# One x tile turned by the crossbar instead of TensorE, a gate vector read as rows, a later weight load, and another engine at the last wait

## The chip, the core and the metric

The kernel runs on one core of a Trainium2 chip. The core has five engines, each with an instruction list of its own that it works off in order: TensorE (PE, with PEld for its weight loads), VectorE (DVE), ScalarE (ACT), GpSimd (POOL) and SyncE (SP), which only issues transfers. Transfers run on 16 DMA engines that all queues share; SyncE's are q1 in the profile, ScalarE's q10, GpSimd's q0. Engines wait for each other through semaphores. The metric is the device time of one execution in microseconds; smaller is better. The time before is 260.21 us, the median of three runs (259.76 to 260.26).

## The reference

Two blocks read the same `x` (2048 tokens of 640 features, bfloat16), and a gate per token mixes their results:

```python
x = A_x
g = _sigmoid((x * gate_w).sum(-1, keepdims=True))
a = _A_ref(x, A_wqkv, A_wo)                     # linear attention, 32 heads of 20
b = _B_ref(x, B_w1, B_w2, B_w3, B_w4)           # mixer with shifted columns, then an MLP of 1728
return g * a + (1 - g) * b

# A: q, k, v = x @ wqkv;  phi(t) = where(t > 0, t + 1, exp(t)) + 1e-6
#    kv = phi(k)^T v, z = sum phi(k), o = phi(q) kv / (phi(q) z + 1e-6), a = o @ wo
# B: h = gelu(layernorm(x) @ w1); four column groups of h are shifted by 1 or 2 tokens; x1 = x + h_shifted @ w2
#    b = x1 + gelu(layernorm(x1) @ w3) @ w4
```

## The kernel before, in words

The tokens are cut into 16 tiles of 128 (`t`), and four chunks of 512 (`c`); the 640 features into five pieces of 128 (`k`). Everything stays in SBUF. `_Sched` records every operation with what it reads and writes, works out the semaphore waits, and emits one instruction list per engine. The order of the work is set by `_Items.run`, a planner with a cost model: it keeps streams of items (name, duration, dependencies with lags) and always takes the item that could start first on TensorE by its model. An item's function emits its instructions, its transfers too, at that place of the engines' lists.

The stages, in order of time:
- Loads and warm-up. Before the planner starts, the transfers of the beginning are written out by hand: ScalarE's queue loads the first piece of wq; SyncE's loads x tiles 0 to 2, wq's second piece, x tile 3, the other wq pieces, the five pieces of `wkg`, the gate vector, then the x chunks of tiles 4 to 15. TensorE multiplies constants meanwhile.
- Queries and keys of block A. Products need x with features on partitions, `xT`. Tiles 0 to 3 are turned by TensorE (`t_x`: five transposes into PSUM, line 617, and a VectorE copy, line 671), tiles 4 to 15 by the crossbar: a transposing transfer from SyncE's queue (line 703). `q_four` does the queries of tiles 0 to 3 as one stream, whose order of steps is a list written by hand: `(t, k)` is the product of tile t with piece k of wq (lines 893 and 894), `(t, None)` turns tile t. Then `k_first` (line 914) and `k_tile` do the keys; `wkg` has 642 columns read there: the keys' 640, one of ones and one with the gate vector, so that a row sum and the gate's product come with the keys. ScalarE takes exponentials, VectorE finishes phi.
- Block A's small matrices (`gt_step`, line 812, `kvt_group`, `lt_evac`, `m_quads`), and layer norm 1: GpSimd normalizes a tile, SyncE turns it by the crossbar into `xnT`.
- Products with w1 and w2 (`w1_group`, `w2_tile`), layer norm 2 in the same way (`n2`, `t2`: item `("t2", u)` is the transposing transfer of tile u), products with w3 (`w3_group`, `w3_half`, line 1120) and w4 (`w4_enter`, lines 1208 and 1213, `w4_tile`, line 1233), with block A's output products (`a_tile`) in between. Weight loads w3 and w4 are items of the planner on SyncE's queue (`w3_load`, `w4_load`).
- Outputs: transfers to HBM from SyncE's queue and, for a part of the last tile, ScalarE's.

At the end `emit` appends the waits for the outputs' landings to SyncE's list, and a barrier of all engines closes the program. The function `stream` has a case `(None, None)`, which the order of `q_four` does not use before; it held a short warm-up.

Of the kernel before, what the change touches and what calls it, by code (L numbers as in the profile page):

```python
# [5 lines left out]
BF16 = mybir.dt.bfloat16  # L6
F32 = mybir.dt.float32
ACTF = mybir.ActivationFunctionType
# [3 lines left out]
D = 640  # L12
# [3 lines left out]
NT = S // 128  # L16
NCH = S // 512
KD = D // 128
# [33 lines left out]
class _Sched:  # L52
# [247 lines left out]
    def emit(self):  # L300
        nc = self.nc
        with ExitStack() as es:
            sems = {}
            for e in ("pe", "act", "dve", "pool"):
                sems["c:" + e] = es.enter_context(nc.semaphore("cnt_" + e))
            for k in self.dma_cnt:
                sems["d:" + k] = es.enter_context(nc.semaphore("dma_" + k))
            seen = {w for p in self.prog.values() for (waits, _fn, _sem) in p for w in waits}
            last = {k: i for i, k in enumerate(self.out_order)}
            left = [k for k in self.dma_cnt if k not in last and ("d:" + k, 16 * self.dma_cnt[k]) not in seen]  # L310
            for k in sorted(last, key=last.get, reverse=True) + left:
                self.prog["sp"].append(([("d:" + k, 16 * self.dma_cnt[k])], None, None))
            engs = {"pe": nc.tensor, "act": nc.scalar, "dve": nc.vector, "pool": nc.gpsimd, "sp": nc.sync}

            for name, e in engs.items():
                for (waits, fn, sem) in self.prog[name]:
                    for (sk, val) in waits:
                        e.wait_ge(sems[sk], val)
                    if fn is not None:
                        fn(e).then_inc(sems[sem], 16 if sem.startswith("d:") else 1)  # L320
            nc.all_engine_barrier()
# [95 lines left out]
def _build(nc, A_x, A_wqkv, A_wo, B_w1, B_w2, B_w3, B_w4, gate_w, out, dbg=None, stop=None):  # L417
    sch = _Sched(nc)
# [37 lines left out]
    pa = Arena(SB_LO, SB_HI - SHARED)  # L456
# [3 lines left out]
    ps = nc.alloc_psum_tensor("ps", [128, 8, 512], F32)  # L460
# [6 lines left out]
    ident = pa.alloc("ident", [128, 128], BF16)  # L467
# [11 lines left out]
    x_tok = pa.alloc("x_tok", [128, NT, D], BF16)  # L479
# [10 lines left out]
    junk = pa.alloc("junk", [128, 1, D], BF16)  # L490
    qprod = pa.alloc("qprod", [128, D], F32)
    zacc = qprod
    zsum = pa.alloc("zsum", [128, D], BF16)
    zT = ones_c[:, :].rearrange("p (k f) -> p k f", f=128)
    zf = pa.alloc("zf", [128, KD], BF16)
    xT = ra.alloc("xT", [128, KD, S], BF16)
    GT = ra.alias("GT", [128, KD, D], BF16, ra.last_addr, KD * S * 2)
    wkg = ra.alloc("wkg", [128, KD, NK], BF16)
# [21 lines left out]
    def bank():  # L520
        best = None
        for k_ in range(nbanks[0]):
            b = (bank_rr[0] + k_) % nbanks[0]
            if b in bank_pend or b in bank_hold:
                continue
            lk = sch.locks.get(b)
            tfree = 0.0 if lk is None else sch.ev_time.get((lk[1].sem, lk[1].val), 1e18)
            if best is None or tfree < best[0]:
                best = (tfree, b)
        bank_rr[0] = best[1] + 1  # L530
        bank_pend.add(best[1])
        return best[1]
# [67 lines left out]
    def mm_group(out_ap, pairs, reads_extra=()):  # L600
        n = len(pairs)

        def fn(e, out_ap=out_ap, pairs=pairs, n=n):
            ins = None
            for i, (l, r) in enumerate(pairs):
                ins = e.matmul(out_ap, l, r, start=(i == 0), stop=(i == n - 1))  # L606
            return ins
        reads = [a for p in pairs for a in p] + list(reads_extra)
        return pe(fn, reads, [out_ap], cost=n * (max(nfree(pairs[0][1]), 24) * 0.4167 + 2.5))
# [39 lines left out]
    def activation(out_ap, in_ap, func, scale=1.0, bias=0.0, accum=None):  # L649
        rd = [in_ap] + [a for a in (scale, bias) if not isinstance(a, (int, float))]  # L650
        wr = [out_ap] + ([accum] if accum is not None else [])
        n = nfree(out_ap)
        cost = max(150.0, 100.0 + 0.833 * n + (70.0 if in_psum(in_ap) else 0.0)) + 45.0 * (len(rd) - 1)
        if accum is not None:
            cost += 91.0
        st_ = ACT_SET.get(func)
        if st_ is not None and st_ != sch.act_func:
            cost += 1290.0
            sch.act_func = st_
        if accum is not None:  # L660
            return act(lambda e: e.activation(out_ap, in_ap, func, bias=bias, scale=scale, accum_out=accum), rd, wr, cost=cost)  # L661
        return act(lambda e: e.activation(out_ap, in_ap, func, bias=bias, scale=scale), rd, wr, cost=cost)  # L662
# [4 lines left out]
    def copy(engf, out_ap, in_ap):  # L667
        cost = None
        if engf is dve and in_ap.dtype == BF16 and out_ap.dtype == BF16:
            cost = 65.0 + nfree(out_ap) / 1.92  # L670
        return engf(lambda e: e.tensor_copy(out_ap, in_ap), [in_ap], [out_ap], cost=cost)  # L671
# [7 lines left out]
    def dma_in(out_ap, in_ap, key, **kw):  # L679
        return sch.dma("sp", out_ap, in_ap, key, **kw)  # L680
# [4 lines left out]
    def load_wq(k, queue="sp"):  # L685
        sch.dma(queue, wq[:, k, :], A_wqkv[128 * k:128 * (k + 1), 0:D], "wq%d" % k)

    memset(pool, wkg[:, :, D:D + 2], 1.0)
    load_wq(0, "act")
    for t in range(3):  # L690
        load_x(t)
    load_wq(1)
    load_x(3)
    for k in range(2, KD):
        load_wq(k)
    for k in range(KD):
        dma_in(wkg[:, k, 0:D], A_wqkv[128 * k:128 * (k + 1), D:2 * D], "wk%d" % k)
    dma_in(wkg[:, :, D + 1:D + 2], gate_w.rearrange("(k p o) -> p k o", p=128, o=1), "gw", noncontig=True)
    for c in range(1, NCH):
        for u in {1: (1,), 2: (2, 3)}.get(c, ()):  # L700
            dma_in(x_tok[:, 4 * u:4 * u + 4, :], x2[512 * u:512 * (u + 1), :].rearrange("(n p) d -> p n d", p=128), "xc%d" % u)
        for t in range(4 * c, 4 * c + 4):
            sch.dma("sp", xT[:, :, 128 * t:128 * (t + 1)], x_tok[:, t, :], "trx%d" % (t % 4), transpose=True)

    k_done = {}

# [47 lines left out]
    IT = _Items()  # L754
    WARM = 3072
    WARM2 = 128
# [97 lines left out]
    def warmup(cols, cyc):  # L854
        b = bank()
        steps = [512] * (cols // 512) + [128] * (cols % 512 // 128)

        def fn(e):
            ins = None
            for n in steps:  # L860
                ins = e.matmul(ps[:, b, 0:n], one(128), one(n), start=True, stop=True)
            return ins
        pe(fn, [], [ps[:, b, :]], cost=cols * cyc)
# [13 lines left out]
    def stream(order, w, n2, done):  # L877
        bs = {}
        for t, k in order:
            if k is None:  # L880
                if t is None:
                    warmup(WARM2, 0.42)
                else:
                    t_x(t)
                continue
            if k == 0:
                bs[t] = pair()
                bank_hold.update((bs[t], bs[t] + 1))
            b = bs[t]
            l = xT[:, k, 128 * t:128 * (t + 1)]  # L890

            def fn(e, l=l, b=b, k=k):
                e.matmul(ps[:, b, 0:512], l, w[:, k, 0:512], start=(k == 0), stop=(k == KD - 1))  # L893
                return e.matmul(ps[:, b + 1, 0:n2], l, w[:, k, 512:512 + n2], start=(k == 0), stop=(k == KD - 1))  # L894
            pe(fn, [w[:, k, 0:512 + n2], l], [ps[:, b, 0:512], ps[:, b + 1, 0:n2]], cost=272.0)
            if k == KD - 1:
                bank_hold.difference_update((b, b + 1))
                done(t, b)

    def q_four():  # L900
        order = [(0, 0), (1, None), (2, None), (1, 0), (0, 1), (1, 1), (2, 0), (2, 1), (3, None), (0, 2), (1, 2), (0, 3), (0, 4), (1, 3),
                 (1, 4), (2, 2), (2, 3), (2, 4), (3, 0), (3, 1), (3, 2), (3, 3), (3, 4)]
        stream(order, wq, 128, lambda t, b: phi(b, pq_tok[:, t + 1, :]))

    def k_out(t, b):
# [370 lines left out]
    for c in range(NCH):  # L1276
        for j in range(KD):
            deps = [(("t1", u), 0.9) for u in range(4 * c, 4 * c + 4)] if j == 0 else []
# [6 lines left out]
    for t in range(NT):  # L1285
        c = t // 4
        deps = [(("w1", c, KD - 1), GEL)]
# [8 lines left out]
    for u in range(NT):  # L1296
        deps = [(("s2", u // 4), 3.2 + 0.9 * (u % 4))]
# [4 lines left out]
        IT.add("N2", ("n2", u), 0.0, lambda u=u: normalize(2, u, st2), deps)  # L1302
        IT.add("T2", ("t2", u), 0.0, lambda u=u: t_xn(2, u), deps=[(("n2", u), 1.1)])
    IT.add("MISC", ("w3load",), 0.0, w3_load, deps=[(("k", NT - 1), 0.0), (("t1", NT - 1), 0.0)])
    IT.add("MISC", ("w4load",), 0.0, w4_load, deps=[(("kvt",), 0.0), (("t1", NT - 1), 0.0), (("z", NT - 1), 1.5)])
    for c in range(NCH):
        for j in range(KFF):
            deps = []
# [4 lines left out]
            if j == 0:  # L1313
                deps = deps0 + [(("t2", u), 0.9) for u in range(4 * c, 4 * c + 4)]
# [11 lines left out]
    for t in range(NT):  # L1326
        deps = [(("zb",), 1.0), (("qr", max(t // 4, 1)), 2.0)]
# [48 lines left out]
    order = IT.run(sch, hook)  # L1376
# [42 lines left out]
```

## Time and profile before

| What | Value |
|---|---|
| Median of three runs | 260.21 us (259.76 to 260.26) |
| Profiled execution | 260.06 us |
| Span of its trace, first to last instruction | 258.3 us |
| Busy: TensorE, VectorE, ScalarE, GpSimd | 254.8, 158.2, 110.9, 96.8 us |
| Granted TensorE clock | 1.000 |
| Moved by DMA | 26.78 MB |

The span is what the views of the trace divide; the 1.8 us around it are start and end of the program outside its instructions. A timeline row has the start in us, the duration, engine, line, operation, what is written and read, how many instructions are merged, and in brackets the idle time before and who ended it. A DMA row has the median time from issue to landing at its end. A row of the chain is a piece of the path that ended last. A row of a window has, behind the stretch, each engine's busy time and number of instructions, and then the granted clock, the share of the DMA engines' time and GB/s.

### The profile page before, as it was taken

The numbers are of one execution on the slowest core, as the hardware profiler recorded it, in microseconds if no ns is written. First come the engines' busy times: TensorE is split into PE (matmuls) and PEld (weight loads), VectorE is DVE, ScalarE is ACT, GpSimd is POOL, SyncE is SP. The second block draws the span as 40 slices with busy tenths as digits, with TensorE's granted clock in tenths as the row PEclk, the third lists the DMA queues.
The fourth block names the chain that finished last, engine by engine and source line by source line (L and its number), as shares of the span: only waits on it lengthen the run. The fifth ranks groups of instructions, "written<-read, shape, count | busy, mean of one in ns | idle before, by whom it ended". The sixth has DMA issues, their size and how long they took to land.

```text
span 258.3 us, 3824 instructions
## 1 busy us (share of the span) xinstructions
PE 254.8 (99%) x1427; PEld 122.7 (47%) x1427; DVE 158.2 (61%) x293; ACT 110.9 (43%) x229; POOL 96.8 (37%) x154
## 2 busy tenths in 40 slices
PE   7999999999999999999999999999999999999996
PEld 3555555544444554554444444444444444444443
DVE  2597877899954699989995302999022530134076
ACT  1496777751355857684874240005500045200100
POOL 8014996869934119659681210111020120021000
DMA  6857997826527699483668512114200140000224
GB/s 194 263 101 235 139 141 193 231 55 119 102 49 105 124 392 305 82 101 65 127 124 117 102 20 23 25 25 130 42 3 0 20 124 0 0 0 1 43 84 139
DMA packets 58644, 26.78 MB, mean 104 GB/s; under 512 B 49966, under 2 KB 57215, under 8 KB 58626
## 3 DMA queue, kind: packets, MB, share of 16 engines
q1 hardware_dynamic: 57122, 22.92, 42.5%
q0 software_dynamic: 1168, 3.28, 5.4%
q10 hardware_dynamic: 336, 0.35, 0.4%
q8 instruction: 11, 0.18, 0.3%
q14 instruction: 7, 0.06, 0.1%
HBM read 12.09 MB, written 2.67 MB: 57 GB/s over the span
## 4 chain that ended last, share of the span: by engine, by line
PE 97%; DMA 1%; DVE 0%; issue 0%
PE ps L606 61%; PE ps L1233 22%; PE ps L812 7%; PE ps L893 2%; PE ps L792 1%; DMA x_tok<-in_A_x_dram 1%; PE ps L1120 1%; PE ps L1208 1%; PE ps L617 1%; PE ps L914 1%; PE ps L894 0%; PE ps L984 0%; PE ps L793 0%; PE ps L1213 0%; PE ps L1017 0%; DVE xT L671 0%
## 5 line engine op out<-in xcount | busy, mean ns | idle before, releaser
L606 PE MATMUL ps<-xnT,w 128*128 128x512 bf16 x360 | 81.3, 379 | 0.0
L606 PEld LDWEIGHTS ps<-xnT,w 128*128 128x128 bf16 x360 | 34.6, 98 | 39.3
L645 DVE SCALAR_TENSOR_TENSOR x_tok<-ps,stg,abx 128x512 bf16<-128x512 f32 (+2 forms) x17 | 12.2, 718 | 58.5 <-PE ps L1233 58.4
L1233 PE MATMUL ps<-w,h2T 128*128 128x512 bf16 (+2 forms) x221 | 47.2, 366 | 0.0
L628 POOL TENSOR_SCALAR abx<-x_tok,stg 128x512 f32<-128x512 bf16 x16 | 12.0, 753 | 88.2 <-DVE x_tok L645 70.1
L628 POOL TENSOR_SCALAR xn<-x_tok,st 128x640 bf16<-128x640 bf16 x32 | 38.6, 1215 | 8.6 <-DMA xnT<-xn 8.2
L662 ACT ACTIVATE h2T<-ps 128x512 bf16<-128x512 f32 x52 | 29.9, 599 | 22.7 <-PE ps L606 22.6
L1233 PEld LDWEIGHTS ps<-w,h2T 128*128 128x128 bf16 x221 | 21.2, 98 | 24.1
L662 ACT ACTIVATE tlT<-ps 128x512 bf16<-128x512 f32 x8 | 4.8, 597 | 64.1 <-PE ps L606 41.9
L662 ACT ACTIVATE Er<-ps 128x640 bf16<-128x640 f32 (+1 forms) x35 | 22.9, 658 | 17.8 <-PE ps L606 9.7
L661 ACT ACTIVATE junk<-x_tok 128x640 bf16<-128x640 bf16 x32 | 23.6, 737 | 4.7 <-DVE x_tok L643 4.2
L662 ACT ACTIVATE hsT<-ps 128x512 bf16<-128x512 f32 (+1 forms) x32 | 18.9, 593 | 14.2 <-PE ps L606 13.8
L606 PE MATMUL ps<-w,hsT 128*128 128x512 bf16 (+1 forms) x160 | 24.0, 299 | 0.0
L606 PE MATMUL ps<-wkg,xT 128*128 128x512 bf16 (+1 forms) x150 | 22.6, 299 | 0.0
L606 PE MATMUL ps<-M_sb,pqnT 128*128 128x512 bf16 x80 | 19.7, 379 | 0.0
L606 PEld LDWEIGHTS ps<-w,hsT 128*128 128x128 bf16 x160 | 13.4, 98 | 12.5
L645 DVE SCALAR_TENSOR_TENSOR abx<-ps,stg,abx 128x512 f32<-128x512 f32 x16 | 12.0, 750 | 10.7 <-PE ps L606 7.2
L606 PEld LDWEIGHTS ps<-wkg,xT 128*128 128x128 bf16 x150 | 12.6, 97 | 11.7
L643 DVE SCALAR_TENSOR_TENSOR x_tok<-ps,x_tok 128x640 bf16<-128x640 f32 x16 | 13.1, 821 | 7.6 <-PE ps L606 6.9
L812 PE MATMUL ps<-pk_tok,x_tok 128*128 128x512 bf16 x80 | 17.8, 379 | 0.0
L636 DVE TENSOR_TENSOR qprod<-qprod,pk_tok 128x640 f32<-128x640 f32 x13 | 16.3, 1252 | 0.5
L628 DVE TENSOR_SCALAR Er<-Er 128x640 bf16<-128x640 bf16 (+1 forms) x35 | 11.6, 332 | 7.6 <-ACT Er L662 6.8
(85 smaller groups left out, 282.9 us busy)
## 6 DMA issues: line engine op xcount, KB each, us to landing
w<-in_B_w_dram SPq DMA_DIRECT2D x1, 2160.0 KB, 9.5
w<-in_B_w_dram SPq DMA_DIRECT2D x1, 2080.0 KB, 15.0
x_tok<-in_A_x_dram SPq DMA_DIRECT2D x3, 640.0 KB, 5.6
out_dram<-x_tok SPq DMA_DIRECT2D x3, 640.0 KB, 3.5
w<-in_B_w_dram POOLq DMA_DIRECT2D x8, 160.0 KB, 6.2
wkg<-in_A_wqkv_dram SPq DMA_DIRECT2D x5, 160.0 KB, 3.9
wv<-in_A_wqkv_dram POOLq DMA_DIRECT2D x1, 800.0 KB, 5.6
x_tok<-in_A_x_dram SPq DMA_DIRECT2D x4, 160.0 KB, 3.2
```

Source lines behind the costliest of these rows:

```text
L606: ins = e.matmul(out_ap, l, r, start=(i == 0), stop=(i == n - 1))
L617: ins = e.transpose(o, s_, ident[:])
L628: return engf(lambda e: e.tensor_scalar(out_ap, in_ap, s1, s2, op0, op1), rd, [out_ap], cost=cost)
L636: return engf(lambda e: e.tensor_tensor(out_ap, a, b_, op), [a, b_], [out_ap], cost=cost)
L643: return dve(lambda e: e.scalar_tensor_tensor(out_ap, in0, scalar, in1, op0, op1, accum_out=accum), rd, [out_ap, accum], cost=cost + 70.0)
L645: return dve(lambda e: e.scalar_tensor_tensor(out_ap, in0, scalar, in1, op0, op1), rd, [out_ap], cost=cost)
L661: return act(lambda e: e.activation(out_ap, in_ap, func, bias=bias, scale=scale, accum_out=accum), rd, wr, cost=cost)
L662: return act(lambda e: e.activation(out_ap, in_ap, func, bias=bias, scale=scale), rd, wr, cost=cost)
L792: e.matmul(ps[:, b, :], l, x_tok[:, t, 0:512], start=(t == 0), stop=(t == NT - 1))
L812: ins = e.matmul(ps[:, b, :], l, r, start=(t0 + q_ == 0), stop=(t0 + q_ == NT - 1))
L893: e.matmul(ps[:, b, 0:512], l, w[:, k, 0:512], start=(k == 0), stop=(k == KD - 1))
L1233: ins = e.matmul(o, l, r, start=False, stop=(i == KFF - 1), skip_group_check=shared)
```

## The change

There are four parts.
- x tile 3 is turned by a transposing transfer from ScalarE's queue instead of TensorE and VectorE. A one-column exponential ahead of it makes ScalarE load its table first. SyncE's transposes of tiles 4 to 15 wait for it (`deps=[turned3]`). The hand-written order of `q_four` loses `(3, None)`, and `(2, 2)` moves ahead.
- The gate vector is read from ScalarE's queue as five contiguous rows of 128 into a new tile `gw5`, instead of element by element into column 641 of `wkg`. A new step `gate_turn`, fourth in `q_four`'s order, turns it with one TensorE product against the identity, and VectorE copies the result into that column.
- The item that loads w4 waits for other items, `("ms",)` (the M rows sent to HBM) and `("t2", 7)`, instead of `("t1", 15)` and `("z", 15)`, so that it comes later in SyncE's queue.
- The waits for the outputs' landings are appended to GpSimd's list instead of SyncE's.

```diff
             for k in sorted(last, key=last.get, reverse=True) + left:
-                self.prog["sp"].append(([("d:" + k, 16 * self.dma_cnt[k])], None, None))
+                self.prog["pool"].append(([("d:" + k, 16 * self.dma_cnt[k])], None, None))
...
+    gw5 = pa.alloc("gw5", [KD, 128], BF16)
...
     load_wq(0, "act")
+    sch.dma("act", gw5[:, :], gate_w.rearrange("(k p) -> k p", p=128), "gw")
     for t in range(3):
         load_x(t)
...
+    activation(junk[:, 0, 0:1], nc.const_aps.tensor(1.0, [128, 1], BF16), ACTF.Exp)
+    turned3 = sch.dma("act", xT[:, :, 384:512], x_tok[:, 3, :], "tr3", transpose=True)
     for k in range(KD):
         dma_in(wkg[:, k, 0:D], A_wqkv[128 * k:128 * (k + 1), D:2 * D], "wk%d" % k)
-    dma_in(wkg[:, :, D + 1:D + 2], gate_w.rearrange("(k p o) -> p k o", p=128, o=1), "gw", noncontig=True)
...
-            sch.dma("sp", xT[:, :, 128 * t:128 * (t + 1)], x_tok[:, t, :], "trx%d" % (t % 4), transpose=True)
+            sch.dma("sp", xT[:, :, 128 * t:128 * (t + 1)], x_tok[:, t, :], "trx%d" % (t % 4), transpose=True, deps=[turned3])
...
                 if t is None:
-                    warmup(WARM2, 0.42)
+                    gate_turn()
...
+    def gate_turn():
+        b = bank()
+        mm_group(ps[:, b, 0:KD], [(gw5[:, :], ident[0:KD, 0:KD])])
+        copy(dve, wkg[:, :, D + 1:D + 2], ps[:, b, 0:KD].unsqueeze(2))
+
     def q_four():
-        order = [(0, 0), (1, None), (2, None), (1, 0), (0, 1), (1, 1), (2, 0), (2, 1), (3, None), (0, 2), (1, 2), (0, 3), (0, 4), (1, 3),
-                 (1, 4), (2, 2), (2, 3), (2, 4), (3, 0), (3, 1), (3, 2), (3, 3), (3, 4)]
+        order = [(0, 0), (1, None), (2, None), (None, None), (1, 0), (0, 1), (1, 1), (2, 0), (2, 1), (0, 2), (1, 2), (2, 2), (0, 3), (1, 3),
+                 (0, 4), (1, 4), (2, 3), (2, 4), (3, 0), (3, 1), (3, 2), (3, 3), (3, 4)]
...
-    IT.add("MISC", ("w4load",), 0.0, w4_load, deps=[(("kvt",), 0.0), (("t1", NT - 1), 0.0), (("z", NT - 1), 1.5)])
+    IT.add("MISC", ("w4load",), 0.0, w4_load, deps=[(("kvt",), 0.0), (("ms",), 0.0), (("t2", 7), 0.0)])
```

## The prediction

> **What bounds the kernel now.** I read the page first, then the chain, the timeline of the first 14 us by engine, the DMA landings of single issues, the waits of SyncE's queue, and the last microseconds.
>
> ```profile
> span 258.3 us, 3824 instructions
> PE 254.8 (99%) x1427; PEld 122.7 (47%) x1427; DVE 158.2 (61%) x293; ACT 110.9 (43%) x229; POOL 96.8 (37%) x154
> PE 97%; DMA 1%; DVE 0%; issue 0%
> ```
>
> TensorE is busy for 254.8 of 258.3 us and carries 97% of the chain. So an edit gains only by taking instructions off TensorE, by closing one of its few gaps, or at the tail; it loses by opening a gap. The change touches the chain in the first 12 us and behind the last output; the w4 load is off it.
>
> ```profile
> 4.96 0.94 PE L617 MATMUL ps<-ident,x_tok 128*128 128x128 bf16 x10
> 6.21 0.39 PE L893 MATMUL ps<-wq,xT 128*128 128x512 bf16 x1 [0.31 <-DVE xT L671]
> 7.58 0.44 PE L617 MATMUL ps<-ident,x_tok 128*128 128x128 bf16 x5
> 7.86 0.38 PE L893 MATMUL ps<-wq,xT 128*128 128x512 bf16 x1
> 10.30 0.38 PE L893 MATMUL ps<-wq,xT 128*128 128x512 bf16 x1
> 7.74 0.28 PE ps L617 x5
> ```
>
> Five rows are from the timeline, the last from the chain. After a gap of 0.31 us (a wait for VectorE's copy) TensorE runs without a stop from 6.21. The five transposes of tile 3 sit inside that run and cost it 0.28 us. The row at 10.30 is the first product of tile 3, (3,0): nine steps after 7.86, 0.271 us each.
>
> **Tile 3, what is removed.** Five transposes go: -0.28 us, because nothing idles on TensorE around them. VectorE's copy behind them (the row at 8.06 below) goes too and gains nothing: it is off the chain. In the new order tile 2's products fill in, and (3,0) is wanted at 10.30 - 0.28 = 10.02. The wq pieces still come first: the third is issued at 3.12, takes about 4.0 (median of the four) and is in by 7.2, while (0,2) moves from 7.86 to 7.58; piece 3 is wanted at 6.21 + 8 x 0.271 = 8.38, as before, piece 4 a little later than before.
>
> ```profile
> 8.06 0.49 DVE L671 COPY xT<-ps 128x640 bf16<-128x640 bf16 x1 [1.51 <-PE ps L617]
> 3.12 1.39 SPq L289 DMA_DIRECT2D wq<-in_A_wqkv_dram  x3
> wq<-in_A_wqkv_dram SPq DMA_DIRECT2D x4, 160.0 KB, 4.0
> ```
>
> **Tile 3, what is added.** One crossbar transfer, which cannot start before x tile 3 is in, and (3,0) now waits for its landing.
>
> ```profile
> 2.65 0.43 SPq L289 DMA_DIRECT2D x_tok<-in_A_x_dram  x1
> x_tok<-in_A_x_dram SPq DMA_DIRECT2D x1, 160.0 KB, 4.1
> xT<-x_tok SPq DMA_TRANSPOSE x1, 2.6
> xT<-x_tok SPq DMA_TRANSPOSE x1, 4.3
> 13.20:18.70 5.50, 5.50 (x39) 3.02 (x38) 4.97 (x11) 5.47 (x16) 0.26 (x1) 1.00 0.47 93
> 6.80:9.50 2.70, 2.70 (x26) 1.64 (x25) 0.49 (x1) 0.35 (x1) 0.28 (x1) 1.00 1.02 329
> ```
>
> Tile 3 lands at 2.65 + 4.1 = 6.75, so ScalarE issues at about 6.8. Alone, the transfer takes 2.6 (issued at 13.22): landing at 9.4, 0.6 before it is wanted, no stall. Beside weight loads of GpSimd's queue it took 4.3 (issued at 25.76): landing at 11.1, a stall of 1.1. Which is nearer? The window rows give the DMA share in the column before the last. From 6.8 to 9.5 the 16 engines are full (1.02) with the weights of SyncE's queue; so this transfer shares, unlike the one at 13.22. Its own work: four transfers fill 0.47 of 5.5 us, 0.65 us of all engines each. If the two queues get half of the time each while both have work, 0.65 becomes 1.3 and it lands 0.65 later, at 10.05. That they can get equal shares is seen where ScalarE's first load (q10) met SyncE's (q1), from 2.66 to 3.1:
>
> ```profile
> q10 hardware_dynamic: 70, 0.09, 57.3%
> q1 hardware_dynamic: 66, 0.08, 47.0%
> 3.73 0.05 issue
> ```
>
> I take that: 10.05 plus 0.05 (the chain's "issue" piece behind the first landing, the last row), against 10.02: a stall of 0.1 us. The sum for tile 3 is -0.28 + 0.10 = -0.18, with ends -0.28 (2.6) and +0.8 (4.3).
>
> The Trainium skill has a rule that speaks against this edit: "DMA: Bandwidth & Descriptors", section "Issuing engines are not separate DMA queues", says that transfers issued on several engines run on the same 16 DMA engines and interleave, so another queue only saves issue time. The q10 and q1 rows agree. The same page, "Queues, rings and completion order", says that an engine changes queues at packet ends, a packet being some 9 to 17 descriptors; by it the transfer would go in about three packets for each engine and wait for as many of the loads, and the sum would come near -0.28 (an estimate). No row here shows how a transfer's packets are grouped.
>
> **What queues behind it.** ScalarE is held by the wait and by the issue (on SyncE 5.48 us for four, 1.4 each), until about 8.2. Its next work is the first exponential:
>
> ```profile
> 1.24 1.28 ACT L662 ACT_TABLE_LOAD   x1 [1.24 <-PEq L1404]
> 9.15 2.06 ACT L662 ACTIVATE Er<-ps 128x640 bf16<-128x640 f32 x3 [6.62 <-PE ps L894]
> 13.22 5.48 SPq L285 DMA_TRANSPOSE xT<-x_tok  x4
> 11.82 1.36 PE ps L914 x10
> ```
>
> That is over 0.9 us of cover, and the new order ends tile 0 two steps later. The added one-column activation keeps the table load early; both end by 3.2, in idle time. SyncE's transposes now also wait for tile 3's, but they start at 13.22, when the x chunk lands; by then it is in, even at 11.1. The loads that yield to it (0.65 us at most) are wkg's, first read by the step at 11.82.
>
> **The gate.** Removed: SyncE's issue at 6.93, and a load of single elements that lands after 4.6; the x chunk behind it is issued 0.48 us earlier. Nobody waits for either at the time. Added: a load behind wq's first piece on ScalarE, issued at 1.25 once that one's 0.41 us are over; one TensorE product of five columns; one small VectorE copy.
>
> ```profile
> 6.93 0.43 SPq L288 DMA_DIRECT2D wkg<-in_gate_w_dram  x1
> wkg<-in_gate_w_dram SPq DMA_DIRECT2D x1, 1.2 KB, 4.6
> 0.80 0.41 ACTq L289 DMA_DIRECT2D wq<-in_A_wqkv_dram  x1
> out_dram<-x_tok SPq DMA_DIRECT2D x1, 32.0 KB, 1.5
> 5.66 0.89 DVE L671 COPY xT<-ps 128x640 bf16<-128x640 bf16 x2 [0.71 <-PE ps L617]
> ```
>
> The landing lies between 1.5 (the smallest transfer of the trace) and 4.6 after the issue, at 2.8 to 5.9; with five rows instead of 640 elements I take 3, at 4.3. The product comes after the ten transposes, which end at 5.90, and TensorE then idles for 0.31 anyway, so a product of under 0.1 costs nothing. If the load came after 6.1, each 0.1 would cost 0.1. The copy follows the two of 5.66, in VectorE's idle time. I take 0.
>
> **The w4 load.** Before, it stands right behind w3 in a burst at 88; now it is behind the M rows and tile 7's transpose on SyncE, at about 115.3.
>
> ```profile
> 88.12 8.38 SPq L289 DMA_DIRECT2D w<-in_B_w_dram  x4
> 114.66 0.56 SPq L289 DMA_DIRECT2D m_rows<-Mt  x1
> 118.91 1.33 SPq L285 DMA_TRANSPOSE xnT<-xn  x1
> 132.66 5.76 SPq L285 DMA_TRANSPOSE xnT<-xn  x4
> w<-in_B_w_dram SPq DMA_DIRECT2D x1, 2080.0 KB, 15.0
> 150.68 2.28 PE ps L1120 x20
> 152.96 0.21 PE ps L1213
> ```
>
> At worst (15.0, behind w3 then) it lands at 130.3, and its first reader is the step at 152.96: 22 us of cover. The four transposes from 118.91 queue behind it. The last four of the sixteen are issued by 138.4 and, with 4.3 for the landing, are in by 142.7; the step at 150.68 reads them, so they have 8 us of cover. What goes is a full SyncE queue at 88 to 97, which TensorE didn't wait for. So 0.
>
> **The end.** The last output is issued at 256.57 and lands 1.5 later, at 258.07; 0.2 of span follows. GpSimd's waits have nothing behind them but the barrier; the instruction ahead of them in its list is tile 15's `abx`, an input of the last VectorE step and so done by then. The hand-over can gain at most those 0.2 and lose about as much: I take 0, +-0.2.
>
> ```profile
> 256.57 0.34 SPq L289 DMA_DIRECT2D out_dram<-x_tok  x1
> ```
>
> **Sum.** -0.28 + 0.10 = -0.18. The profiled execution took 260.06 (span 258.3 and 1.8 around it), so 259.9; the median of the three runs is 260.21, 0.15 above it, so I give 260.0.
>
> **Rivals.**
> B, slower: a wait takes the transposes' place. Queues may alternate packet by packet whatever the size.
>
> ```profile
> DMA packets 2027, 0.51 MB, mean 93 GB/s; under 512 B 2026, under 2 KB 2026, under 8 KB 2026
> DMA packets 862, 0.89 MB, mean 329 GB/s; under 512 B 168, under 2 KB 862, under 8 KB 862
> ```
>
> These are the two windows (13.2 to 18.7, 6.8 to 9.5). A transfer of 160 KB in packets of 0.51 MB / 2027 = 250 bytes has some 640, 40 for each engine, of 0.65 us / 40 = 16 ns; a loading engine passes a large one in 1.02 x 2.7 x 16 / 694 = 63 ns. Alternating, 40 pairs take 40 x 79 ns = 3.2 us instead of 0.65, and the landing is 2.5 later: 11.9, a stall of 1.9, net +1.6: 261.8. The milder case is 4.3: net +0.8, 261.0. It decides from a landing at 10.8 on (0.28 + 0.5 after 10.02). For it: the engines are full, and a row of this kernel shows 4.3. Against it: that row is of another queue and of smaller pieces.
> C, faster by more: no stall (2.6), and the hand-over at the end gains 0.2 to 0.25: -0.5, 259.7 by the median. Against it: the engines are full.
> D, slower elsewhere: the w4 load holds SyncE as the burst at 88 did (8.4 us), and with the queue behind it tile 15's transpose comes later than 150.68; or the gate's rows land after 6.1. Each would cost about 1 us: 261.0. The covers above speak against both.
> That the edits change nothing because TensorE didn't wait is the case of w4 and the gate, and is in the sum.
>
> **How the numbers follow.** The forecast (landing by 10.5, net -0.4 to +0.3) gets 0.45, B 0.33, C 0.12, D 0.10. A change of 0.2%, 0.52 us, is about what a measurement can tell from none. Faster by more than that: 0.03 of the forecast and all of C, 0.15. Slower: B less its mildest part, and D, with a little of the forecast's spread: 0.43. Same: 0.42. The range reaches from 259.6, just under C's 259.7, to 261.6, short of B's far end alone; the forecast's own is 259.8 to 260.5.
>
> **What would show it.** Right: no L617 row at 7.7; q10 with one transfer more; the tile 3 transfer issued at 6.8 and landing at 9.4 to 10.5; (3,0) at 10.0 to 10.4 and TensorE closed up behind it; TensorE at L1213 about 0.2 earlier. Wrong: an idle row before (3,0) that names the DMA into xT, over 0.8 long; an idle row before the gate's product; any new wait between 118 and 153; over 0.4 from the last landing to the end.

## The result, and the profile after

| | Before | After |
|---|---|---|
| Median, six runs each | 260.06 us (259.76 to 260.26) | 268.37 us (266.52 to 269.16) |
| Profiled execution, span | 260.06, 258.3 us | 268.37, 266.6 us |
| Granted TensorE clock | 1.000 | 0.984 |

The ratio is 1.0313 (95% interval 1.0279 to 1.0347): the change costs 8.3 us, far outside the range of the prediction. The head of the program lost 6.3 us and its end 2.0. Among the six runs the two with a granted clock of 0.994 took 266.52 and 267.69, the four with 0.984 or 0.985 took 268.36 to 269.16: a part of the loss varies, and the clock varies with it. First the page of after: span, busy time, the granted clock in 40 slices of 6.67 us, and the chain by engine.

```profile
span 266.6 us, 3793 instructions
PE 255.7 (96%) x1396; PEld 123.4 (46%) x1423; DVE 158.2 (59%) x293; ACT 111.0 (42%) x230; POOL 96.8 (36%) x154
PEclk9959999999999999999999999999999999999998
PE 77%; DVE 11%; DMA 5%; ACT 2%; issue 1%; SPq 1%; DVEq 0%
```

TensorE is busy 0.9 us longer although five transposes are gone, and the third slice (13.3 to 20.0) has half the clock. DMA has 5% of the chain where it had 1%. Next the timeline of after around tile 3's transfer and, in a fence of its own, three pieces of its chain: start, duration, what.

```profile
6.58 1.34 ACTq L285 DMA_TRANSPOSE xT<-x_tok  x1
...
6.95 0.43 SPq L289 DMA_DIRECT2D x_tok<-in_A_x_dram  x1
...
9.99 0.22 PE L897 MATMUL ps<-wq,xT 128*128 128x128 bf16 x1
14.13 0.61 PE L896 MATMUL ps<-wq,xT 128*128 128x512 bf16 x1 [3.92 <-DMA xT<-x_tok]
...
14.64 0.63 PE L896 MATMUL ps<-wq,xT 128*128 128x512 bf16 x1
```

```profile
6.58 7.50 DMA xT<-x_tok
...
16.98 2.52 PE ps L922 x10
...
262.51 0.35 DVE x_tok L646
```

The transfer is issued as foreseen and takes 7.50 us, not 2.6 to 4.3. The product (3,0) begins at 14.13 behind a wait of 3.92, where before it began at 10.30: 3.83 later. Then its pairs follow each other by 0.51 to 0.54 us instead of 0.27, and the ten key products take 2.52 instead of 1.36. From (3,0) to the end of these ten it is 14.13 to 19.50, 5.37 us; before, 10.30 to 13.18, 2.88. That is 2.49 more. 3.83 + 2.49 = 6.32, which is also how much later the last VectorE step starts: 262.51 against 256.19, in the row of before's chain that comes next. So the stages between add nothing on balance.

```profile
256.19 0.35 DVE x_tok L645
```

The end, by the instructions of the line of the final barrier: duration in ns three times (shortest, median, longest), then the start in us. First VectorE, SyncE and GpSimd after, then GpSimd and SyncE before.

```profile
L321 DVEq DRAIN  x1: 389/389/389, 262.5 to 262.5; - x1
...
L321 SPq DRAIN  x1: 136/136/136, 263.3 to 263.3; - x1
L321 POOLq DRAIN  x1: 2028/2028/2028, 264.4 to 264.4; - x1
```

```profile
L321 POOLq DRAIN  x1: 2797/2797/2797, 233.2 to 233.2; - x1
...
L321 SPq DRAIN  x1: 13/13/13, 258.1 to 258.1; - x1
```

Each engine empties itself at the barrier. Before, SyncE waited for the outputs, and its drain behind the wait took 13 ns; GpSimd's, 2.80 us long, began at 233.2 and nobody saw it. After, GpSimd's drain begins when the last output has landed (264.4, 1.9 behind the last VectorE step, as SyncE's did before) and lasts 2.03 us. From the last VectorE step to the end of the span it was 258.3 - 256.19 = 2.1 us and is 266.6 - 262.51 = 4.1.

Tile 3's transfer doesn't travel by itself. The issues of after and before, with the landing time at the end: the x chunk that SyncE issues 0.37 us behind it has become later too.

```profile
x_tok<-in_A_x_dram SPq DMA_DIRECT2D x1, 640.0 KB, 7.3
xT<-x_tok ACTq DMA_TRANSPOSE x1, 7.5
```

```profile
x_tok<-in_A_x_dram SPq DMA_DIRECT2D x1, 640.0 KB, 5.8
```

Both transfers end within 0.2 us of each other, at 14.1 and 14.3.

Together: the wait 3.83, the half rate 2.49 and GpSimd's drain 2.0 make 8.3, the whole of the loss.

### The profile page after: what moved, and what is told of

It reads as the page before. It is cut to its first block, busy times and chain, and to the rows that moved or that the text cites. A ratio compares the mean times of both kernels' runs of the same rounds, so it can differ in the third digit from the quotient of the medians.

```text
span 266.6 us, 3793 instructions
## 1 busy us (share of the span) xinstructions
PE 255.7 (96%) x1396; PEld 123.4 (46%) x1423; DVE 158.2 (59%) x293; ACT 111.0 (42%) x230; POOL 96.8 (36%) x154
## 4 chain that ended last, share of the span: by engine, by line
PE 77%; DVE 11%; DMA 5%; ACT 2%; issue 1%; SPq 1%; DVEq 0%
PE ps L607 51%; PE ps L1241 21%; DVE qprod L637 7%; DMA xT<-x_tok 3%; DVE x_tok L644 2%; DMA x_tok<-in_A_x_dram 1%; ACT h2T L663 1%; DMA xnT<-xn 1%; PE ps L922 1%; PE ps L795 1%; PE ps L896 1%; PE ps L1128 1%; DVE pq_tok L1155 1%; PE ps L1216 1%; SPq L289 1%
## 5 line engine op out<-in xcount | busy, mean ns | idle before, releaser
L607 PE MATMUL ps<-xnT,w 128*128 128x512 bf16 x350 | 79.9, 379 | 0.7 <-DMA xnT<-xn 0.2
L1241 PE MATMUL ps<-w,h2T 128*128 128x512 bf16 (+2 forms) x215 | 46.4, 366 | 0.3
L663 ACT ACTIVATE hsT<-ps 128x512 bf16<-128x512 f32 (+1 forms) x32 | 18.9, 593 | 14.2 <-PE ps L607 13.8
L607 PE MATMUL ps<-w,hsT 128*128 128x128 bf16 (+1 forms) x159 | 23.8, 298 | 0.1
L607 PE MATMUL ps<-wkg,xT 128*128 128x130 bf16 (+1 forms) x149 | 22.5, 298 | 0.1
L607 PEld LDWEIGHTS ps<-w,hsT 128*128 128x128 bf16 x160 | 13.4, 98 | 12.5
## 6 DMA issues: line engine op xcount, KB each, us to landing
w<-in_B_w_dram SPq DMA_DIRECT2D x1, 2080.0 KB, 11.2
```

Source lines behind the costliest of these rows:

```text
L1241: ins = e.matmul(o, l, r, start=False, stop=(i == KFF - 1), skip_group_check=shared)
```

## The experiments

The theory, T in the expectations: the transposing transfer on ScalarE's queue crawls while SyncE's queue has loads, weights and then the x chunk, and TensorE idles for it; the idling drops its clock to half for some microseconds; GpSimd's drain adds 2.0 at the end; the gate and the w4 load are worth nothing. Each R is a rival, told where it stands. All medians are set beside runs of the kernel before on the same chip.

**The waits alone on GpSimd** (`e1_pool_only`), in the kernel before:

```diff
-                self.prog["sp"].append(([("d:" + k, 16 * self.dma_cnt[k])], None, None))
+                self.prog["pool"].append(([("d:" + k, 16 * self.dma_cnt[k])], None, None))
```

> The kernel before with one edit: the waits for the outputs stand in GpSimd's list instead of SyncE's. Theory T (the barrier's drain of GpSimd, 2.03 us in the trace after and 2.80 us at 233 us in the trace before, now starts only behind the last landing): the tail is 2.0 us longer, 262.1 us (261.8 to 262.5), with a row of GpSimd's drain of about 2 us right behind its waits. Rival R (the longer tail after comes with the late start or the lower clock, not with the engine that waits): 260.1 us, the tail as before.

Measured: 262.09 us (261.86 to 262.14) against 260.13, ratio 1.0072 [1.0057, 1.0087]: 2.0 us. The barrier's line shows the drain behind the wait.

```profile
L321 POOLq DRAIN  x1: 2028/2028/2028, 257.9 to 257.9; - x1
```

**After, with the waits back on SyncE** (`e2_after_sp_waits`): the line above, turned round.

> The changed kernel with that edit alone undone: the waits stand in SyncE's list again. Theory T: 268.4 - 2.0 = 266.4 us (265.5 to 267.2), the span ends 0.3 us or less after the last landing. Rival R: 268.4 us.

Measured: 265.86 us, ratio 1.0236 [1.0200, 1.0271]; three of the four runs took 265.74 to 265.93 at a granted clock of 0.994, the fourth 267.74 at 0.987. With e1 this adds up to 5.7 + 2.0 = 7.7 of the 8.3. The other 0.6 is the clock's: in e2's profiled execution it is half from 15.57 to 18.98, 3.41 us of work, in after's TensorE works at half rate from 14.13 to 19.21, 5.08 us. Half of the difference is 0.83, less the 0.21 by which e2's wait ends later. Its timeline shows the half rate as a thing apart from the wait.

```profile
14.34 0.39 PE L896 MATMUL ps<-wq,xT 128*128 128x512 bf16 x1 [4.11 <-DMA xT<-x_tok]
...
15.17 0.38 PE L896 MATMUL ps<-wq,xT 128*128 128x512 bf16 x1
...
15.44 0.51 PE L896 MATMUL ps<-wq,xT 128*128 128x512 bf16 x1
...
15.85 2.88 PE L922 MATMUL ps<-wkg,xT 128*128 128x512 bf16 x10
```

For 1.1 us after the wait the products run at the full pitch of 0.27; from 15.44 on they take double, and the ten key products end at 18.7. In after the half rate was there with the first product.

**The waits on ScalarE** (`e8_act_waits`), in the kernel before: is it any engine but SyncE, or GpSimd?

```diff
-                self.prog["sp"].append(([("d:" + k, 16 * self.dma_cnt[k])], None, None))
+                self.prog["act"].append(([("d:" + k, 16 * self.dma_cnt[k])], None, None))
```

> The kernel before with one edit: the waits for the outputs stand in ScalarE's list instead of SyncE's. Theory T (what counts is how long the barrier's drain of the waiting engine takes; ScalarE's took 0.15 us at the end of the trace before, SyncE's 0.01): 260.2 us, at most 0.2 over the kernel before. Rival R7 (any engine but SyncE pays some 2 us when it waits for transfers): 262 us.

Measured: 260.17 us against 260.13, ratio 1.0002 [0.9993, 1.0011]. It is GpSimd's drain, not the move: ScalarE's behind the same waits takes 8 ns.

```profile
L321 ACTq DRAIN  x1: 8/8/8, 258.2 to 258.2; - x1
```

**Tile 3 alone** (`e3_tile3_only`): the kernel before with the transfer on ScalarE's queue and the new order without the gate's step; the gate is loaded element by element from SyncE's queue as before.

```diff
+    activation(junk[:, 0, 0:1], nc.const_aps.tensor(1.0, [128, 1], BF16), ACTF.Exp)
+    turned3 = sch.dma("act", xT[:, :, 384:512], x_tok[:, 3, :], "tr3", transpose=True)
...
-            sch.dma("sp", xT[:, :, 128 * t:128 * (t + 1)], x_tok[:, t, :], "trx%d" % (t % 4), transpose=True)
+            sch.dma("sp", xT[:, :, 128 * t:128 * (t + 1)], x_tok[:, t, :], "trx%d" % (t % 4), transpose=True, deps=[turned3])
...
-        order = [(0, 0), (1, None), (2, None), (1, 0), (0, 1), (1, 1), (2, 0), (2, 1), (3, None), (0, 2), (1, 2), (0, 3), (0, 4), (1, 3),
+        order = [(0, 0), (1, None), (2, None), (1, 0), (0, 1), (1, 1), (2, 0), (2, 1), (0, 2), (1, 2), (2, 2), (0, 3), (1, 3),
```

> The kernel before with tile 3 turned by the crossbar from ScalarE's queue and q_four's new order, nothing else; the gate vector is still read element by element on SyncE's queue. Theory T (the crossbar transfer interleaves with the loads of the other queue and lands only when they do): lands about 7 us after its issue, TensorE waits about 4 us before (3,0) and then runs at half rate for some 5 us; 260.06 + 6.3 = 266.4 us (265 to 268). Rival R2 (the new gate load ahead of it on the same queue, or SyncE's x chunk that is issued 0.48 us earlier without the old gate load, is what delays it): landing after 4 to 5 us, 262 us or less.

Measured: median 263.02 us of five runs, some 3 us less than expected. Three of them (261.76 to 263.02) kept a granted clock of 1.000, the profiled one took 263.78 at 0.993, and one took 267.42 at 0.987, as low as after's and within what was expected; 1.0096 [1.0066, 1.0126] is the ratio of the other four. In the profiled execution the transfer landed after 5.6, not about 7, the wait was 2.02, and the half rate came 0.8 us after it.

```profile
xT<-x_tok ACTq DMA_TRANSPOSE x1, 5.6
wkg<-in_gate_w_dram SPq DMA_DIRECT2D x1, 1.2 KB, 5.3
```

```profile
12.33 0.39 PE L895 MATMUL ps<-wq,xT 128*128 128x512 bf16 x1 [2.02 <-DMA xT<-x_tok]
...
13.15 0.58 PE L895 MATMUL ps<-wq,xT 128*128 128x512 bf16 x1
...
13.64 0.63 PE L895 MATMUL ps<-wq,xT 128*128 128x512 bf16 x1
```

What differs from after is on SyncE's queue: the element load of the gate stands between the wkg loads and the x chunk, which is issued 0.5 us later (7.46 against 6.95). The gate's rows on ScalarE's queue, the other half of R2, are no candidate: in after TensorE turns them from 5.88 on, so they had landed before the transfer was issued at 6.58. So what SyncE issues behind the transfer matters, the chunk above all; e10 takes that up.

**Keep TensorE busy in the wait** (`e5_keep_warm`): after, with 16 products of constants ahead of (3,0).

```diff
+                if t == "warm":
+                    warmup(8192, 0.2167)
...
-                 (0, 4), (1, 4), (2, 3), (2, 4), (3, 0), (3, 1), (3, 2), (3, 3), (3, 4)]
+                 (0, 4), (1, 4), (2, 3), (2, 4), ("warm", None), (3, 0), (3, 1), (3, 2), (3, 3), (3, 4)]
```

> The changed kernel with 16 constant products of 512 columns (3.5 us) put into TensorE's wait, right before (3,0); nothing else moves. Theory T (of the loss at the head, 4 us are the wait and up to 2.6 us the half rate at which TensorE runs after it, because it idled): the wait for the transfer is as long as before, about 10.0 to 14.1, but the products of tile 3 follow each other every 0.27 us as in the trace before, not every 0.54; the time is up to 2.6 us less, 265.8 us (265.4 to 266.6), and the runs lie closer together. Rival R4 (the products behind the wait are slow for another reason, such as the transposes and loads that land in SBUF beside them): 268.4 us, still every 0.54.

Measured: 266.50 us (265.91 to 266.59), 1.9 below after although the transfer landed still later (8.2 after its issue) and (3,0) began 0.66 later than in after. The wait that is left is 1.44, and then everything has the full pitch.

```profile
14.79 0.39 PE L898 MATMUL ps<-wq,xT 128*128 128x512 bf16 x1 [1.44 <-DMA xT<-x_tok]
...
15.07 0.38 PE L898 MATMUL ps<-wq,xT 128*128 128x512 bf16 x1
...
16.16 1.53 PE L924 MATMUL ps<-wkg,xT 128*128 128x512 bf16 x10
```

Sixteen products that compute nothing made the kernel faster: the half rate comes from idling.

**Hold SyncE's loads** (`e6_loads_held`): after, but the wkg loads and the first x chunk wait for tile 3's transfer.

```diff
-        dma_in(wkg[:, k, 0:D], A_wqkv[128 * k:128 * (k + 1), D:2 * D], "wk%d" % k)
+        dma_in(wkg[:, k, 0:D], A_wqkv[128 * k:128 * (k + 1), D:2 * D], "wk%d" % k, deps=[turned3])
...
-            dma_in(x_tok[:, 4 * u:4 * u + 4, :], x2[512 * u:512 * (u + 1), :].rearrange("(n p) d -> p n d", p=128), "xc%d" % u)
+            dma_in(x_tok[:, 4 * u:4 * u + 4, :], x2[512 * u:512 * (u + 1), :].rearrange("(n p) d -> p n d", p=128), "xc%d" % u, deps=[turned3])
```

> The changed kernel with the five wkg loads and the first x chunk held on SyncE's queue until tile 3 is turned, so that the crossbar transfer has at most wq's last pieces beside it. Theory T (the loads beside it are what slows it): lands 2.6 to 3.3 us after its issue, by 10.0, and no wait or under 0.3 us before (3,0); the keys then wait for wkg instead, so the time says little. Rival R5 (a transposing transfer from ScalarE's queue, or the first one of the program, is slow by itself): 5 us or more as before.

Measured: 265.33 us (264.27 to 266.40), ratio 1.0199 [1.0159, 1.0239]. The transfer took 2.7 and landed at 9.68, before it was wanted; TensorE waited for wkg instead, and tiles 4 to 7 came later. The waits of TensorE up to 20 us, and the landing:

```profile
PE ps L922 <- DMA wkg<-in_A_wqkv_dram: 1.5, 3, 0.6
```

```profile
xT<-x_tok ACTq DMA_TRANSPOSE x1, 2.7
```

So ScalarE's queue is not slow in itself, and issuing from it isn't: the rival stated there falls. The loads beside it are the cause.

**The same transfer from SyncE's queue** (`e7_sp_queue`): after, with it between the wkg loads and the x chunk.

```diff
-    turned3 = sch.dma("act", xT[:, :, 384:512], x_tok[:, 3, :], "tr3", transpose=True)
     for k in range(KD):
         dma_in(wkg[:, k, 0:D], A_wqkv[128 * k:128 * (k + 1), D:2 * D], "wk%d" % k)
+    turned3 = sch.dma("sp", xT[:, :, 384:512], x_tok[:, 3, :], "tr3", transpose=True)
```

> The changed kernel with tile 3's crossbar transfer issued from SyncE's queue, behind the fifth wkg load and ahead of the x chunk, instead of from ScalarE's. Theory T (it is the packet-wise mixing of transposes with the loads of another queue that slows both; in one queue they go one after the other): lands about 1 us behind the fifth wkg load, at 11 to 11.7, 4.3 to 4.8 us after its issue; a wait of 1 to 1.7 us, no half rate behind it, 268.4 - 4.5 = 263.9 us (263 to 264.5; the waits are still GpSimd's). Rival R6 (any load in flight slows a transpose, whatever the queue): landing at 13.5 or later, 267 us or more.

Measured: 263.06 us (262.81 to 263.32), ratio 1.0112 [1.0096, 1.0128]. It is issued 0.36 us later than in after and lands 2.6 earlier, at 11.52; the wait is 1.39, with no half rate after it. The chunk behind it is faster too.

```profile
x_tok<-in_A_x_dram SPq DMA_DIRECT2D x1, 640.0 KB, 5.0
xT<-x_tok SPq DMA_TRANSPOSE x1, 4.6
```

```profile
11.57 0.39 PE L896 MATMUL ps<-wq,xT 128*128 128x512 bf16 x1 [1.39 <-DMA xT<-x_tok]
...
12.94 1.52 PE L922 MATMUL ps<-wkg,xT 128*128 128x512 bf16 x10
```

The engines are as full here: the windows from 7.0 to 11.5 have a DMA share of 1.09 in both (the column before the last; after first, this kernel second). So full engines alone don't make it crawl, and the rival stated there falls. One thing is not separated: the transfer's issue holds SyncE for 1.29 us, so the chunk is issued at 8.28 instead of 6.95. How much of the gain comes from the shared queue and how much from the later chunk no run shows.

```profile
7.00:11.50 4.50, 3.16 (x23) 1.69 (x22) 1.29 (x3) 1.90 (x3) 0.09 (x1) 1.00 1.09 285
```

```profile
7.00:11.50 4.50, 3.13 (x23) 1.67 (x22) 1.33 (x3) 1.90 (x3) 0.10 (x1) 1.00 1.09 269
```

**Hold the x chunk alone** (`e10_chunk_held`): of e6's edit the second part only; the wkg loads run beside the transfer.

> The changed kernel with the first x chunk alone held on SyncE's queue until tile 3 is turned; the five wkg loads still run beside the transfer. Theory T (packets of loads and of the transpose share the engines as long as loads are queued): the transfer lands about when the last wkg load does, at 10.7 to 11.7, 4 to 5 us after its issue, between the 2.7 of the run with all loads held and the 7.5 of the changed kernel. Rival R8 (the x chunk alone delays it): by 10, as in the run with all held. Rival R9 (the wkg loads are what delays it): 13 or later.

Measured: 262.99 us (262.96 and 263.03), ratio 1.0111 [1.0093, 1.0130]. The transfer lands at 11.14, 0.6 behind the last wkg load, and the wait is 0.86.

```profile
xT<-x_tok ACTq DMA_TRANSPOSE x1, 4.2
```

```profile
11.19 0.39 PE L896 MATMUL ps<-wq,xT 128*128 128x512 bf16 x1 [0.86 <-DMA xT<-x_tok]
```

Both rivals fall: it is neither the chunk alone nor the wkg loads alone. With the wkg loads beside it the transfer ends just behind them, and in after just before the chunk: there it ends about when the other queue's work does. In e3, where the chunk was issued later, it ended well before it (12.3 against 13.9). The prices in order: alone 2.7, beside wkg 4.2, beside wkg and the chunk 7.5.

**Gate and w4 without tile 3** (`e4_gate_and_w4`): after with tile 3 turned by TensorE in the old order, the gate's step fourth, and SyncE's waits.

```diff
+        order = [(0, 0), (1, None), (2, None), (None, None), (1, 0), (0, 1), (1, 1), (2, 0), (2, 1), (3, None), (0, 2), (1, 2), (0, 3), (0, 4), (1, 3),
+                 (1, 4), (2, 2), (2, 3), (2, 4), (3, 0), (3, 1), (3, 2), (3, 3), (3, 4)]
```

> The changed kernel with tile 3 turned by TensorE again, in the old order with the gate's step added, and the waits in SyncE's list: only the gate rows and the later w4 load remain. Theory T: 260.1 us (259.8 to 260.4), no wait on TensorE. Rival R3 (the gate's rows or the later w4 load cost something that the other waits hide): over 260.6 us, with a new idle row on TensorE.

Measured: 262.19 us (261.76 to 264.09), ratio 1.0091 [1.0056, 1.0125], 2 us more than expected. TensorE's waits that before didn't have are these:

```profile
6.87 0.39 PE L894 MATMUL ps<-wq,xT 128*128 128x512 bf16 x1 [0.75 <-DMA wq<-in_A_wqkv_dram]
...
12.60 0.39 PE L894 MATMUL ps<-wq,xT 128*128 128x512 bf16 x1 [1.75 <-DVE pq_tok L646]
```

The second and larger is of my making: the gate's product takes a PSUM bank from the rotation, every later step gets the next one, and with the old order (3,0) got one that VectorE had not finished. The first, for wq's second piece, I can't tie to the edit.

**The same without the shift of banks** (`e9_gate_w4_bank`): the step right before `(3, None)`, in a bank that isn't in use there.

```diff
     def gate_turn():
+        bank_rr[0] = 7
         b = bank()
```

> Again only the gate rows and the later w4 load, as in the run of that name, which had a wait of 1.75 us before (3,0) for VectorE: the added step had taken a PSUM bank and so shifted which banks tile 3's products got. Here the gate's step stands right ahead of tile 3's transposes and takes bank 7, so that all other steps have the banks of the kernel before. Theory T: that wait is gone and nothing takes its place, 260.1 to 260.4 us. Rival R3 (the gate rows or the w4 load cost something by themselves): 260.8 us or more, with an idle row on TensorE that names a DMA.

Measured: 260.29 us (ten runs, 260.05 to 260.69) against 260.25, ratio 1.0002 [0.9992, 1.0011]. The gate's rows and the later w4 load cost and bring nothing that the runs can tell. The edit moves the step as well as its bank: it shows that e4's loss belonged to neither the gate's rows nor the w4 load; that it was the bank is read from the kernel. Of TensorE's waits these are not among before's:

```profile
PE ps L607 <- DMA xnT<-xn: 0.2, 1, 0.2
PE ps L607 <- ACT h2T L663: 0.2, 1, 0.2
```

They are 0.2 us each, within what the runs differ by, and none is at the gate's step or at w4's readers.

**Want tile 3 later** (`e11_tile3_late`): if the transfer can't come by 10, its readers can be moved. The transfer is SyncE's as in e7, the waits SyncE's, and the queries of tile 3 come behind the keys of tiles 0 to 2.

```diff
-                 (0, 4), (1, 4), (2, 3), (2, 4), (3, 0), (3, 1), (3, 2), (3, 3), (3, 4)]
+                 (0, 4), (1, 4), (2, 3), (2, 4)]
...
+    def q_late():
+        stream([(3, k) for k in range(KD)], wq, 128, lambda t, b: phi(b, pq_tok[:, t + 1, :]))
...
+        if i == 3:
+            addA(("q3",), 1.36, q_late)
```

> A version that should keep the gain and drop the losses: gate rows and later w4 load as changed; waits in SyncE's list; tile 3 turned by the crossbar from SyncE's queue between the last wkg load and the x chunk (landing at 11.5 in the run that did this); and the queries of tile 3 moved behind the keys of tiles 0 to 2, so that they are wanted at about 14.1 instead of 10.0. Theory T: no wait on TensorE, five transposes less, 260.2 - 0.3 = 259.9 us (259.6 to 260.1). Rival R10 (the keys of tile 0, now wanted at 10.0, wait for the last wkg loads, which land up to 10.9): 260.3 to 261.

Measured: 260.14 us (eleven runs, 259.50 to 260.66) against 260.13 (259.59 to 261.25), ratio 0.9999 [0.9987, 1.0011]. The interval includes a gain of 0.28 as well as nothing, so this doesn't settle whether the time of the transposes is gained. It does show that the whole loss of 8.3 us can be avoided with the crossbar still in use: tile 3 lands at about 10.9 (3.9 after its issue at 6.95) and is read from 13.8 on.

**The same from ScalarE's queue** (`e12_tile3_late_act`), all else as in e11:

> The same as the version with tile 3's queries behind the keys of tiles 0 to 2, but with the crossbar transfer on ScalarE's queue as in the change. Theory T (mixing the transfer with the loads of the other queue delays both): the transfer lands at 12 to 14.7, the wkg loads 0.3 to 0.8 later than in one queue, and the x chunk 1 us later; TensorE waits for a wkg load at about 10.5 and possibly again for tile 3 at 14; 260.3 to 261.5 us, slower than the version with one queue. Rival R11 (only the place of tile 3's products matters): the same time, within 0.3 us.

Measured: 260.96 us (260.49 to 261.36), ratio 1.0034 [1.0022, 1.0046], slower than e11's 260.14. The transfer takes 8.4 us, the chunk 8.0 (5.8 before), and waits open at other places:

```profile
x_tok<-in_A_x_dram SPq DMA_DIRECT2D x1, 640.0 KB, 8.0
xT<-x_tok ACTq DMA_TRANSPOSE x1, 8.4
```

```profile
PE ps L925 <- DMA wkg<-in_A_wqkv_dram: 0.5, 1, 0.5
PE ps L607 <- DMA xT<-x_tok: 0.3, 1, 0.3
```

So later readers cover the wait for tile 3 but not what the two queues do to the loads: 0.5 + 0.3 = 0.8, which is the difference between the two.

## Why the prediction was wrong, and where it was right

**Wrong: "Tile 3, what is added".** The step took the transfer's own work (0.65 us of all engines), gave each queue half of the time, and got a landing at 10.05 and a stall of 0.1. It landed at 14.09. Equal shares of the time failed: beside full engines of its own queue the transfer took 4.6 (e7), beside another queue's loads 7.5 to 8.4 with the chunk behind them (after, e5, e12), 5.6 with the gate's elements in between (e3), 4.2 without the chunk (e10) and 2.7 with the wkg loads and the chunk held back (e6). The stall of 0.1 was 3.9.

The row taken for equal shares, 57.3% and 47.0% for q10 and q1, could not tell equal time from equal numbers of packets: both queues were loading, with packets of 1.2 to 1.3 KB (0.09 MB in 70, 0.08 MB in 66). The transpose's packets have 250 bytes. In after, in the three half microseconds from 10.5 to 12.0, q10 got 64, 87 and 98 packets and q1 69, 94 and 105, nearly as many, but 20 to 22% of the engines' time against 85 to 96%. So the numbers of packets were shared there, and the time one to four.

The 7.50 can be split by q10's packets. The first started 2.4 us after the issue (e6, alone: 1.3), the data took 3.2 from there (e6: 0.9), and the last of the 32 packets of four bytes that close it started only at 13.64, 1.4 behind the last data packet (e6: 0.02); from 12.5 to 14.0 q10 has six packets in all, while the chunk's go on. The landing followed 0.45 later. So tile 3's data had been sent well before TensorE was told. Why the closing packets stood back no run here shows.

The 0.65 was also misread. The window from 13.2 to 18.7 holds 0.51 MB, that is 3.1 transfers of 160 KB and not four, so one is 0.83 us of all engines; e6's packets alone give 0.84. By the prediction's own rule that moves the landing to 10.2, no more.

The sentence on the Trainium skill's "DMA: Bandwidth & Descriptors", section "Queues, rings and completion order", said that turns by packets of 9 to 17 descriptors would leave the sum near -0.28. The measured landings contradict that use of the rule. The sentence counted the turns and not what they cost: three turns of 9 to 17 load descriptors, at the prediction's 63 ns for each, are 1.7 to 3.2 us (an estimate with the Trainium skill's figure), the size of rival B. Whether the turns were of one packet or of several no run here shows; the nearly equal numbers of packets fit both.

**Wrong in size: rival B.** It named the place, and a mechanism that the numbers of packets fit, queues alternating packet by packet. Its price, landing 11.9 and net +1.6, counted 40 pairs of packets, over after 3.2 us whatever the other queue holds. With the wkg loads alone that is not far off (11.14, e10); with the x chunk of 640 KB, which SyncE issues 0.37 us later, the landing is 14.09, another 2.95. So the far end of the range stood too low.

**Missing: the clock.** No step priced what an idle TensorE does afterwards. It is 2.49 us in the profile of after; the medians of after and e5 differ by 1.9, and e5's (3,0) began 0.66 later, which makes 2.5. The row that shows it is the granted clock's third slice, 5 where all others are 9 but the last. Two windows date the fall, after's first, then e3's; the granted clock is the third column from the end.

```profile
11.50:14.10 2.60, 0.00 (x0) 0.00 (x0) 1.97 (x4) 0.00 (x0) 0.00 (x0) 0.67 0.49 145
```

```profile
11.50:14.10 2.60, 1.77 (x10) 0.87 (x11) 2.06 (x4) 0.00 (x0) 0.00 (x0) 0.83 0.67 214
```

A mean of 0.67 is half the clock for the last 1.7 us: it fell at 12.4, while TensorE still waited. In e3 it fell at 13.2, with TensorE back at work for 0.9 us. Narrower windows show that it was half from 12.39 to 19.21 in after, from 15.57 to 18.98 in e2 and from 13.20 to 16.62 in e3: 3.41 us, or twice that.

The Trainium skill's "TensorE: Matmul & The Clock Gate", Part 1, "What's actually happening", has the rule: half the clock after an idle window of about 3.4 us, full again after as long a busy one. The traces agree in the length, but the window was not idle throughout: in the 3.41 us ahead of the three falls TensorE was busy for 1.18 (after), 1.22 (e2) and 1.33 us (e3). The 3.41 us ahead of those in e2, with 1.44 us of work, had no fall behind them. So what counted was how little TensorE worked in such a stretch, not the length of one wait: this fits the 2.0 us of e3 that were enough, and the drops that came only behind a wait. It is an inference from these few stretches.

**Wrong: "The end".** It allowed +-0.2 for the hand-over and said that GpSimd had nothing behind its waits but the barrier. The barrier begins with a drain, and the trace of before had its length: 2797 ns on GpSimd, hidden at 233.2. The step never looked at the barrier's own line. It costs 2.0 (e1), and ScalarE in GpSimd's place nothing (e8).

**Right: "Tile 3, what is removed".** The last product ahead of (3,0) starts at 9.99 in after, and such a product is followed by the next after 0.06 (its piece in the chain of before): (3,0) could have begun at 10.05, where the step said 10.02 and before had 10.30. So TensorE has the 0.28 less to do, and (3,0) then begins 4.1 later. Whether it shows in the time where no wait is left, e11 doesn't settle.

**Right: the gate and w4.** The gate's load is issued at 1.24, its product and copy fall into the gap before tile 1 and into VectorE's idle time; the w4 load is behind the M rows and lands 11.2 us after an issue by 124.7, at 135.9 at the latest, for a first reader at 159.2 (timeline and issues of after). e9, with the gate's step at another place, measured both together at 1.0002; at its place in after the trace shows no cost, since the product behind it starts at 6.24 where before it started at 6.21.

```profile
5.88 0.17 PE L607 MATMUL ps<-ident,gw 5*128 5x5 bf16 x1
...
6.49 0.17 DVE L672 CAST wkg<-ps 128x5 bf16<-128x5 f32 x1
...
121.58 3.12 SPq L289 DMA_DIRECT2D w<-in_B_w_dram  x3
...
159.21 0.92 PE L1216 MATMUL ps<-w,h2h 64*128 64x512 bf16 x6
```

```profile
w<-in_B_w_dram SPq DMA_DIRECT2D x1, 2080.0 KB, 11.2
```

**Right: ScalarE's cover.** The issue holds ScalarE until 7.92, and no wait of TensorE names an exponential. That SyncE's transposes now wait for tile 3's cost nothing either: the chunk that they need landed at 14.26, after it (and 1.06 later than before's 13.20, which the late TensorE covers).

What stays open: by what unit the DMA engines change between a transposing and a loading queue, why the closing packets came so late, and how little TensorE must work for the clock to fall (these traces leave 1.33 to 1.44 of 3.41 us).

## What to carry to other kernels

A small transfer that TensorE waits for is priced by all that other queues still send while it runs, loads issued after it too: find the last of them on the timeline and take its end, with some tenths of a microsecond more (0.2 in e5, 0.6 in e10), as the transfer's latest landing, or put the transfer into the same queue ahead of the large load. A wait of two microseconds or more on TensorE can have a second price in the slower products behind it (here up to 2.5 us), so price it twice or fill it. Before the last wait of a program is moved to another engine, read that engine's drain on the barrier's line.

## What the hardware showed that was not expected

- A transposing transfer of 160 KB took 2.7 us alone, 4.6 in the queue of the loads, ahead of the large one, and 7.5 to 8.4 beside another queue that went on to the large one; that one became slower too (the x chunk 7.3 to 8.0 instead of 5.8).
- GpSimd's drain at the closing barrier took 2.0 us behind waits for transfers and 2.8 behind its computing; SyncE's and ScalarE's behind such waits took 13 and 8 ns.
- The granted clock fell to half behind 3.41 us in which TensorE had worked for 1.2 to 1.3 us: during the wait (after), or 0.9 and 1.2 us after work had begun again (e3, e2). It came back after 3.41 us or twice that.
- A transfer's data can be sent long before its landing is reported: in after the last data packet started at 12.20 and the last closing packet at 13.64.
